# Sliding-window attention with routed experts: first loads on three queues, and the first expert tiles built earlier

## The chip, the core and the metric

The kernel runs on one core of a Trainium2 chip. A core has TensorE (matrix products; "PE" in the profile, its weight loads "PEld"), VectorE ("DVE"), ScalarE ("ACT"), GpSimd ("POOL") and SyncE ("SP", which here only starts transfers), each with its own instruction stream. They meet through semaphores. Sixteen DMA engines move data between the memory outside (HBM) and the on-chip memory. TensorE writes its products to PSUM, eight banks, from which VectorE or ScalarE copy them. The metric is the device time of one execution in microseconds (us). The kernel before takes 764.41 us, the median of 3 runs (762.5 to 765.28).

## What is computed

```python
# q, k, v: (8, 8, 576, 64); window 64
scores = q @ k.T / 8, kept where 0 <= query - key < 64
x = softmax(scores) @ v                    # -> (4608 tokens, 512)
logits = x @ w_gate                        # 8 experts
e = argmax(logits); gate = softmax(logits)[e]
y[t] = gate[t] * (relu(x[t] @ w1[e]) @ w2[e])   # w1[e] 512 x 1024, w2[e] 1024 x 512
```

Every token goes to one expert only. The kernel works in tiles of 256 tokens of one expert, so it must first know which tokens belong together, fetch their rows of x, and then multiply.

## The kernel before

Attention runs over 16 units (a pair of batches times a pair of heads), three steps each, so N = 48 steps. They are pipelined by hand: while the scores of one step are made, the softmax of the step before is transposed and the product with v of the step before that is under way.

```python
def step(s):
    prs[s + 1] = softened(*masked(s + 1, scored(s + 1)))   # scores (PE), mask and max (DVE), exp (ACT)
    px = weighted(s - 1, pTs.pop(s - 1))                   # times v (PE)
    ripe = logit(s - 3)                                    # x times w_gate (PE)
    pTs[s] = flipped(prs.pop(s))                           # transposes of the softmax (PE)
    divided(s - 1, px)                                     # by the row sums (DVE)
    if s % NST == 0:                                       # NST = 3: a new unit
        u = s // NST
        if u + 3 < NU and (u + 3) % NG == 0: load_rests((u + 3) // NG)
        load_v(u + 2); load_qk(u + 3)                      # loads, three units ahead
    turned(s + 3)                                          # transposes of q and k (PE)
    x_turned(s - 2)                                        # transposes of x (PE)
    for op in todo.pop(s, ()): op()                        # routing work placed by step
```

A sequence has 576 positions: 512 are read by `load_qk` and `load_v`, the last 64, for all heads at once, by `load_rests`. All of these go through SyncE's queue. Loads and steps begin like this:

```python
load_qk(0)
nc.sync.dma_start(out=wg[:, :, 0:E], in_=...)              # w_gate
nc.sync.dma_start(out=x_dram[NT : NT + 1, :], in_=zrow[:])
load_rests(0); load_v(0); load_qk(1); load_v(1); load_qk(2)
for g in range(NG):                                        # w1 of expert 0, in four parts
    step = NST * (g // 2) + g % 2 + 1
    todo.setdefault(step, []).append(partial(nc.scalar.dma_start, out=w1s[0][:, g : g + 1], in_=...))
for n, op in enumerate(left_sums(G, s1s[0], *w1q(0))):     # sums of blocks of w1, on GpSimd
    todo.setdefault(3 * NST + n, []).append(op)
# ...
for s in range(-3, N):
    step(s)
```

After each pair of batches (there are four) `choose` ranks the tokens within their experts on VectorE, `place` writes one-hots of a token's place (two VectorE instructions for each block of 128 tokens), `weigh` multiplies the rows of x by their gate, and `store` writes them to `x_dram`. The expert part then fetches rows from there. A table of places says which token stands where: TensorE multiplies the one-hots `lo` and `hi`, and the result is a list of row numbers. The whole table is ready only when the last pair is ranked. Two tiles of expert 0 are formed earlier, from the first three of the four pairs (27 of the 36 blocks):

```python
# in choose(), pair bg; last = 3, NE = 2, TB = 256
if bg == last - 1:
    V.tensor_scalar_max(count[:, 0:1], count[:, 0:1], float(NE * TB))

# the third pair's work by step; its first step is 39
for n in (0, 0, 1, 2, 2):
    do(n, part)                                            # the five parts of choose()
for m in range(NTB):                                       # NTB = 9 blocks
    do(3 + m // 3, partial(place, bg * NTB + m))
    do((2, 2, 3, 3, 4, 4, 4, 5, 5)[m], partial(weigh, bg, m, nc.scalar if m in (2, 6) else G))
    if m % ST == ST - 1:
        do(3 + m // ST, partial(store, bg, m // ST, G))
do(6, first_tiles)

def first_tiles():                                         # NJE = 27, C = 2
    V.scalar_tensor_tensor(out=key[:], ...)
    V.tensor_tensor(out=hi_e[:], in0=_inner(key[:], NE * C), in1=..., op=ALU.is_equal)
    slots = banks[next(tr_ring)](0, NE * C)
    for j in range(NJE):
        for i in range(2):
            nc.tensor.matmul(slots, lhsT=lo[:, i, j], rhs=hi_e[:, j], ...)
    V.tensor_scalar(out=perm_e[:], in0=slots, ...)         # row numbers of tiles 0 and 1
    gather_first(perm_e[:, 0:C])                           # zero, then an indirect transfer on GpSimd
```

After the last step, tile 0's products fill TensorE while VectorE ranks the last pair. A tile is `hidden` (seven groups of 16 products with w1; `a11` and so on are its blocks, combined so that seven block products do for eight), `turn` (transposes of the next tile's rows) and `output` (seven groups with w2); each `next` gives out one group:

```python
sums_w2(0)                                                 # sums of blocks of w2, on GpSimd
tile0 = chain(hidden(0), turn(), output(0))
px = weighted(N - 1, pTs.pop(N - 1))
form_all(turn())                                           # tile 0's own rows
logit(N - 3); divided(N - 1, px); x_turned(N - 2)
sums_x()
gather_first(perm_e[:, C : 2 * C])                         # tile 1's rows
by_tok = [by_tokens(last, c) for c in range(NST)]
next(by_tok[0]); next(tile0)
logit(N - 2); x_turned(N - 1); next(by_tok[0], None); next(by_tok[1]); next(tile0)
logit(N - 1); next(by_tok[2]); next(by_tok[1], None); next(tile0)
# ... choose(last) between the next groups, weigh_some, then
for _ in range(8):
    next(tile0)
    next(table, None)                                      # slot_table: the whole table of places
gather(perm_i[:, 3 * C : 4 * C])
finish(); scatter(perm_e[:, 0:C])
tile1 = chain(hidden(0), turn(), output(0))
```

`slot_table` multiplies the one-hots of the first 27 blocks, then writes those of the last nine block by block and multiplies them. All other tiles follow the same way, expert by expert.

Of the kernel before, what the change touches and what calls it, by code (L numbers as in the profile page):

```python
# [36 lines left out]
def kernel(  # L37
# [44 lines left out]

    ident = consts.tile([P, P], F32, name="ident")
    make_identity(nc, ident[:])
    GE = 32
# [127 lines left out]
    hi_e = rt.tile([P, NJE, NE * C], BF16, name="hi_e")  # L213
# [23 lines left out]
    ST = 3  # L237
# [39 lines left out]
    def gather_first(tokens):  # L277

        for c in range(C):
            G.memset(xg[c], 0.0)  # L280

            G.indirect_dma_start(
                out=xg[c], out_offset=None, in_=x_dram[0 : NT - BG * S, :],
                in_offset=bass.IndirectOffsetOnAxis(ap=tokens[:, c : c + 1], axis=0),
                bounds_check=NT - BG * S - 1, oob_is_err=False,
            )
# [12 lines left out]
    def turn():  # L299
# [7 lines left out]
    def sums_x():  # L307
# [132 lines left out]
    with tc.manual_schedule(), ExitStack() as held, ExitStack() as brief:  # L440
# [6 lines left out]


        NM = 2 + ST
        mask = consts.tile([P, NM, P], BF16, name="mask")  # L450
        nc.gpsimd.memset(mask[:], 0.0)
        for h in range(2):
            for m0, m1, first in ((0, 1, False), (1, 2, h == 0), (2, NM, False)):
                rows = slice(h * D, (h + 1) * D)
                sel = partial(
                    nc.gpsimd.affine_select, out=mask[rows, m0:m1, :], in_=mask[rows, m0:m1, :], fill=MASKED,
                )
                if first:
                    sel(pattern=[[0, m1 - m0], [-1, P]], compare_op=ALU.is_ge, base=0, channel_multiplier=1)
                else:  # L460
                    sel(pattern=[[0, m1 - m0], [1, P]], compare_op=ALU.is_gt, base=0, channel_multiplier=-1)
                    sel(pattern=[[0, m1 - m0], [-1, P]], compare_op=ALU.is_ge, base=WINDOW, channel_multiplier=1)
# [18 lines left out]
        def load_qk(u):  # L481
            bg, g = units[u]
            qks[u] = [qk_m(((u % 3 + 2) % 3 * 2 + n) * 1024, BG, NV, 2, D) for n in range(2)]
            for i in range(BG):
                for t, src in zip(qks[u], (q, k)):
                    for h in range(2):
                        nc.sync.dma_start(
# [4 lines left out]
        def load_rests(bg):  # L492

            at = 6144 + bg % 2 * 2048
            vr = qk_m(at + 1024, BG, H, D)
            rests[bg] = [qk_m(at, H, D), qk_m(at + 512, H, D), vr]
            for t, src in zip(rests[bg], (q, k)):
                for i in range(BG):
                    nc.sync.dma_start(
                        out=t[i * D : (i + 1) * D], in_=src[bg * BG + i, :, SM:S, :].rearrange("h p d -> p h d")  # L500
                    )
            for i in range(BG):
                nc.sync.dma_start(out=vr[D:P, i], in_=v[bg * BG + i, :, SM:S, :].rearrange("h p d -> p h d"))
# [173 lines left out]
        def choose(bg):  # L677
# [50 lines left out]
            if bg == last - 1:  # L728

                V.tensor_scalar_max(count[:, 0:1], count[:, 0:1], float(NE * TB))  # L730
# [48 lines left out]
        def slot_table(hi):  # L779
# [29 lines left out]
            for j in range(NJE):  # L809
                fill(j)  # L810
            for n in range(NST):
                for m in range(ST):
                    place(NJE + n * ST + m)
                yield
# [18 lines left out]
        def after(s, routing, bg):  # L833
# [14 lines left out]
            for n in (0, 0, 1, 2, 2):  # L848
                do(n, part)
            for m in range(NTB):  # L850
                do(3 + m // 3, partial(place, bg * NTB + m))
                do((2, 2, 3, 3, 4, 4, 4, 5, 5)[m], partial(weigh, bg, m, nc.scalar if m in (2, 6) else G))
                if m % ST == ST - 1:
                    do(3 + m // ST, partial(store, bg, m // ST, G))
            do(6, first_tiles)

        def first_tiles():

            V.scalar_tensor_tensor(
                out=key[:], in0=rkhi[:, 0:NJE], scalar=1.0, in1=oh_all[:, 0, 0:NJE], op0=ALU.add, op1=ALU.mult  # L860
# [209 lines left out]
```

## Time and profile before

| | |
|---|---|
| time, median of 3 runs | 764.41 us |
| span of the profiled execution | 763.5 us |
| TensorE busy | 722.8 us, 95% |
| VectorE, ScalarE, GpSimd busy | 397.0, 268.3 and 357.0 us |
| moved by DMA | 94.48 MB, of 137,616 packets 117,072 under 512 B |
| last score group of attention starts | 206.19 us |
| first product of tile 0, of tile 1 | 218.24 us, 249.66 us |

The profile is one execution in which each instruction has a start and a length. A line of the timeline gives the start, the length, the engine, the line of the kernel, the operation, what it writes and reads, its size, and in brackets how long the engine had been idle before it and what released it. Matmul ends are modelled, so a gap between two of them can be a little longer or shorter than it seems. Some lines of the kernel before to know: L572 is the scores, L539 and L531 the transposes of q and k (L531 those of the rests), L603 those of the softmax, L618 the product with v, L643 the transposes of x, L655 the logits, L869 the one-hots of the first tiles, L303 `turn`, L322 the products with w1, L362 those with w2, L807 the table of places.

### The profile page before, as it was taken

The page shows a single profiled execution, that of the slowest core. Times are in us where ns is not written, and L with a number is a line of the kernel's source. Part 1 is how long each engine was busy: PE and PEld are TensorE (multiplying, and loading weights), DVE is VectorE, ACT ScalarE, POOL GpSimd, SP SyncE. Part 2 cuts the span into 40 slices and gives each one's busy share as a digit, 9 for nine tenths or more (in the row PEclk, how much of TensorE's full clock was granted, in tenths as well). Part 3 has the DMA queues.
Part 4 walks back from the last instruction along what each step waited for, and adds up shares of the span by engine and source line. Part 5 has one row for each costly group of instructions (what it writes and reads, how often), then busy time and mean ns, then how long its engine had stood idle before and what let it go on. Part 6 is the DMA issues. An engine that isn't in the chain of part 4 may idle for free. (4 is left out here: it accounts for less than half of the span.)

```text
span 763.5 us, 18251 instructions
## 1 busy us (share of the span) xinstructions
PE 722.8 (95%) x7018; PEld 651.8 (85%) x7018; DVE 397.0 (52%) x1355; ACT 268.3 (35%) x676; POOL 357.0 (47%) x366
## 2 busy tenths in 40 slices
PE   5999999998899989999999999999999999999995
PEld 3878888887688978988999899899998899988994
DVE  2666998988748554434533452352434452424432
ACT  4778888897634201211220121111220121202220
POOL 5214668485770544546531553663256465262111
PEclk9999999999899999999999999999999999999998
DMA  7998889794513711702501170441161171101101
GB/s 161 210 201 183 190 183 257 175 236 128 181 56 125 276 57 32 264 29 93 203 32 54 48 257 30 141 164 56 44 247 53 35 258 56 41 25 42 43 28 55
DMA packets 137616, 94.48 MB, mean 124 GB/s; under 512 B 117072, under 2 KB 117072, under 8 KB 137490
## 3 DMA queue, kind: packets, MB, share of 16 engines
q1 hardware_dynamic: 127858, 62.16, 29.6%
q0 software_dynamic: 9056, 28.58, 11.3%
q10 hardware_dynamic: 576, 2.10, 0.9%
q8 instruction: 74, 1.21, 0.6%
q14 instruction: 52, 0.43, 0.2%
HBM read 73.94 MB, written 20.45 MB: 124 GB/s over the span
## 5 line engine op out<-in xcount | busy, mean ns | idle before, releaser
L322 PE MATMUL bank<-qk_m,s 128*128 128x128 f32 x1216 | 145.6, 275 | 0.0
L322 PEld LDWEIGHTS bank<-qk_m,s 128*128 128x128 f32 x1216 | 140.5, 192 | 0.1
L322 PE MATMUL bank<-qk_m,w 128*128 128x128 f32 x912 | 112.5, 276 | 10.7 <-DVE v_m L358 7.1
L272 POOL DMA_INDIRECT qk_m<-x_dram,at_g x42 | 44.6, 1061 | 166.3 <-PE bank L303 159.0
L322 PEld LDWEIGHTS bank<-qk_m,w 128*128 128x128 f32 x912 | 106.8, 192 | 15.9 <-issue 15.7
L595 ACT ACTIVATE pr<-pr,mx 128x128 f32<-128x128 f32 x288 | 89.7, 391 | 34.2 <-DVE mx L585 31.8
L358 DVE TENSOR_TENSOR v_m<-bank,v_m 128x256 f32<-128x256 f32 x101 | 40.9, 422 | 110.3 <-PE bank L362 54.8
L585 DVE CUSTOM_DVE_ANT_0 pr<-bank,mask 128x128 f32<-128x128 f32 x288 | 64.4, 286 | 28.2 <-PE bank L572 25.8
L292 POOL DMA_INDIRECT out_dram<-v_m,at_s x42 | 42.4, 1009 | 60.7 <-DVE v_m L358 49.0
L329 ACT COPY qk_m<-bank 128x512 f32<-128x512 f32 x19 | 11.2, 587 | 164.2 <-PE bank L322 135.0
L139 POOL TENSOR_TENSOR s<-w 128x1024 f32<-128x1024 f32 x22 | 52.3, 2377 | 17.6 <-DMA qk_m<-x_dram,at_g 17.6
L362 PE MATMUL bank<-qkT_m,v_m 128*128 128x256 f32 x240 | 54.0, 380 | 1.7 <-DVE v_m L139 1.7
L362 PEld LDWEIGHTS bank<-qkT_m,v_m 128*128 128x128 f32 x240 | 45.4, 190 | 8.6 <-DVE v_m L139 2.5
L513 POOL COPY v_m<-v_m 64x520 f32<-64x520 f32 x32 | 19.8, 618 | 69.3 <-DMA v_m<-in_v_dram 55.1
L362 PE MATMUL bank<-qk_m 128*128 128x256 f32 x224 | 52.1, 380 | 0.0
L618 PEld LDWEIGHTS bank<-v_m,pT 128*64 128x64 f32 x1152 | 41.2, 140 | 11.7 <-DVE xs L632 5.5
L618 PE MATMUL bank<-v_m,pT 128*64 128x65 f32 x1152 | 48.0, 231 | 2.7 <-DVE xs L632 2.7
L362 PE MATMUL bank<-s,v_m 128*128 128x256 f32 x216 | 48.1, 379 | 0.0
L362 PEld LDWEIGHTS bank<-qk_m 128*128 128x128 f32 x224 | 41.5, 190 | 5.5 <-ACT v_m L374 0.4
L362 PEld LDWEIGHTS bank<-s,v_m 128*128 128x128 f32 x216 | 41.0, 190 | 5.6
L572 PE MATMUL bank<-qkT_m 64*64 64x128 f32 x1152 | 45.4, 289 | 0.1
L539 PE MATMUL bank<-ident,qk_m 128*128 128x128 f32 x256 | 35.9, 283 | 8.5 <-DMA qk_m<-in_q_dram 6.3
(167 smaller groups left out, 1223.8 us busy)
## 6 DMA issues: line engine op xcount, KB each, us to landing
w<-in_moe_w_dram SPq DMA_DIRECT2D x11, 2048.0 KB, 9.4
qk_m<-in_q_dram SPq DMA_DIRECT2D x72, 128.0 KB, 3.4
qk_m<-in_k_dram SPq DMA_DIRECT2D x72, 128.0 KB, 3.4
v_m<-in_v_dram SPq DMA_DIRECT2D x64, 128.0 KB, 3.8
qk_m<-in_moe_w_dram SPq DMA_DIRECT2D x3, 2048.0 KB, 15.3
x_dram<-xs POOLq DMA_DIRECT2D x6, 512.0 KB, 4.7
x_dram<-xs POOLq DMA_DIRECT2D x3, 768.0 KB, 5.0
w<-in_moe_w_dram ACTq DMA_DIRECT2D x4, 512.0 KB, 4.4
```

The lines of the kernel that those rows point to most:

```text
L139: op()
L272: G.indirect_dma_start(out=xg[c], out_offset=None, in_=x_dram[:, :], in_offset=bass.IndirectOffsetOnAxis(ap=at_g[:, c : c + 1], axis=0),)
L292: put = G.indirect_dma_start(out=out[:, :], out_offset=bass.IndirectOffsetOnAxis(ap=at_s[:, c : c + 1], axis=0), in_=ys[c], in_offset=None ...
L322: nc.tensor.matmul(acc[:, f, :], lhsT=a[:, g, f * P : (f + 1) * P], rhs=b[:, g, :], start=(first and f == 0 and g == 0), stop=(g == HG - 1 ...
L358: plus = lambda out, a, b: V.tensor_tensor(out=out, in0=a, in1=b, op=ALU.add)
L362: nc.tensor.matmul(acc, lhsT=a[:, f, :], rhs=b[:, f, :], start=(start and f == 0), stop=(stop and f == HF - 1), skip_group_check=True,)
L513: nc.gpsimd.tensor_copy(out=vb[0:D, i].rearrange("p j h d -> p (j h d)"), in_=va[D:P, i].rearrange("p j h d -> p (j h d)"),)
L539: nc.tensor.transpose(out=tr.rearrange("d a b -> d (a b)").rearrange("d (p j) -> d j p", j=NV)[:, j, :], in_=t[:, c, j].rearrange("p h d - ...
L572: nc.tensor.matmul(out_, lhsT=qT[rows, t, a * WINDOW : (a + 1) * WINDOW], rhs=rhs, start=True, stop=True, skip_group_check=True,)
L585: V.tensor_tensor_reduce(out=prs[h][:, m, :], in0=scs[h][:, m, :], in1=mask[:, m0 + m, :], scale=-scale, scalar=-2 * MASKED, op0=ALU.add, ...
L595: nc.scalar.activation(out=y, in_=y, func=AF.Exp, scale=-1.0, bias=mx[:, h, m : m + 1])
L618: nc.tensor.matmul(px[a * D : (a + 1) * D, h, m, :], lhsT=pTs[h][:, m, a * D : (a + 1) * D], rhs=vt[:, h, :], start=True, stop=True, skip_ ...
```

## The change

It has four parts. **First loads:** the loads that open the kernel are ordered by first use and issued by three engines: SyncE, ScalarE (rests of q and k for the first two heads) and GpSimd (rests of the other heads). The opening steps are written out, so that the first scores stand ahead of the second block's transposes, and nine matmuls on zeros run before the first data is there. The masks are built sooner. **w1 of expert 0** is loaded in steps 13, 16, 19 and 22 rather than 1, 2, 4 and 5, and its sums follow in steps 24 to 27. **Tile 0** takes its tokens from the first two pairs of batches, tile 1 from the first three: each has its own one-hots, tile 0's in steps 38 and 39, tile 1's after the last step. Expert 0's count is raised to 256 after the second pair and to 512 after the third, so that a later token never gets a place in a closed tile. Ranking, placing, weighing and storing of the third pair are spread over steps 39 to 45, with the stores on SyncE. **Tile 0's rows** are turned in step 46 and its first product stands in step 47; in the slot table the products of the first 27 blocks come after the places of the sixth of the last nine.

The diff, cut to its core (the masks' code is only moved up; `turn` and `sums_x` take their banks as an argument):

```diff
+    warm = consts.tile([P, 4 * P], BF16, name="warm")
+    nc.vector.memset(warm[:], 0.0)
-    hi_e = rt.tile([P, NJE, NE * C], BF16, name="hi_e")
+    hi_e = rt.tile([P, NJE, C], BF16, name="hi_e")
-    def gather_first(tokens):
+    def gather_first(tokens, rows):
...
-                out=xg[c], out_offset=None, in_=x_dram[0 : NT - BG * S, :],
+                out=xg[c], out_offset=None, in_=x_dram[0:rows, :],
...
-            if bg == last - 1:
-                V.tensor_scalar_max(count[:, 0:1], count[:, 0:1], float(NE * TB))
+            if last - NE <= bg < last:
+                V.tensor_scalar_max(count[:, 0:1], count[:, 0:1], float((bg - last + NE + 1) * TB))
... slot_table
-            for j in range(NJE):
-                fill(j)
             for n in range(NST):
                 for m in range(ST):
                     place(NJE + n * ST + m)
+                if n == 1:
+                    for j in range(NJE):
+                        fill(j)
                 yield
... the third pair
-            for n in (0, 0, 1, 2, 2):
+            for n in (0, 1, 1, 2, 3):
                 do(n, part)
             for m in range(NTB):
-                do(3 + m // 3, partial(place, bg * NTB + m))
-                do((2, 2, 3, 3, 4, 4, 4, 5, 5)[m], partial(weigh, bg, m, nc.scalar if m in (2, 6) else G))
+                do((3, 3, 4, 4, 5, 5, 6, 6, 6)[m], partial(place, bg * NTB + m))
+                do((2, 3, 3, 4, 4, 5, 5, 6, 6)[m], partial(weigh, bg, m, G))
                 if m % ST == ST - 1:
-                    do(3 + m // ST, partial(store, bg, m // ST, G))
-            do(6, first_tiles)
+                    do(4 + m // ST, partial(store, bg, m // ST, nc.sync))
... first_tiles becomes first_tile(n), in two parts
+            nj = (last - NE + n + 1) * NTB                 # 18 blocks for tile 0, 27 for tile 1
+            gather_first(to, nj * P)
... the loads
-        load_qk(0)
+        load_qk(0, nc.sync, nc.sync)
+        load_rests(0, 0, 2, nc.scalar, nc.sync)
+        load_v(0)
+        load_qk(1, nc.sync, nc.sync)
+        load_rests(0, 2, H, G)
         nc.sync.dma_start(out=wg[:, :, 0:E], in_=moe_w_gate.rearrange("(g p) e -> p g e", p=P))
         nc.sync.dma_start(out=x_dram[NT : NT + 1, :], in_=zrow[:])
-        load_rests(0)
-        load_v(0)
-        load_qk(1)
         load_v(1)
-        load_qk(2)
+        load_qk(2, nc.sync, nc.sync)
-            step = NST * (g // 2) + g % 2 + 1
+            step = NST * (NG + g) + 1
...
-            todo.setdefault(3 * NST + n, []).append(op)
+            todo.setdefault(2 * NG * NST + n, []).append(op)
... in step(s): load_rests moves behind load_qk, to s % NST == 1, and
+            if s == 0:
+                turned(2)
... the last steps and the first
-        for n, s in enumerate((N - 6, N - 3)):
+        for n, s in enumerate((N - 7, N - 4)):             # w2 of expert 0
...
+        tile0 = chain(hidden(0), turn(), output(0))
+        first = first_tile(0)
+        todo.setdefault(N - 10, []).append(partial(next, first))
+        todo.setdefault(N - 9, []).append(partial(next, first))
+        free = [banks[i](0, NG, P) for i in (0, 1)]
+        todo.setdefault(N - 2, []).extend((lambda: form_all(turn(free)), partial(sums_x, free)))
+        todo.setdefault(N - 1, []).extend((partial(next, tile0), partial(sums_w2, 0)))
+        for _ in range(9):
+            nc.tensor.matmul(banks[7](0, 4 * P), lhsT=warm[:, 0:P], rhs=warm[:], start=True, stop=True)
+        turned(0)
+        first = masked(0, scored(0))
+        turned(1)
+        prs[0] = softened(*first)
-        for s in range(-3, N):
+        for s in range(N):
             step(s)
-        sums_w2(0)
... after the last step
-        form_all(turn())
...
-        sums_x()
-        gather_first(perm_e[:, C : 2 * C])
+        second = first_tile(1)
+        next(second)
+        next(tile0)
         by_tok = [by_tokens(last, c) for c in range(NST)]
         next(by_tok[0])
-        next(tile0)
         logit(N - 2)
         x_turned(N - 1)
+        next(second)
... and weigh_some(2) moves from before the last eight groups of tile 0 to after the second of them
```

## The prediction

> **What bounds the kernel now.** I read the slices of the page first, then a table of stages, then TensorE's timeline at the two ends of the attention half. The slices say who is busy:
>
> ```profile
> PE   5999999998899989999999999999999999999995
> PEclk9999999999899999999999999999999999999998
> DMA  7998889794513711702501170441161171101101
> ```
>
> TensorE (PE) is the bound nearly everywhere, so time can come back only where PE's row is below 9: slice 1, slices 10, 11 and 15 and the last (a slice is 19.1 us). Slice 11 also has a reduced clock. The diff touches slices 1 to 13. The stages in us (columns: window, its length, then busy time and count for PE, PEld, DVE, ACT, POOL; clock, DMA share, GB/s):
>
> ```profile
> 0.00:24.00 24.00, 15.22 (x138) 11.41 (x139) 7.41 (x53) 11.21 (x28) 9.77 (x36) 0.93 0.79 165
> 24.00:60.00 36.00, 34.40 (x611) 28.52 (x610) 24.12 (x144) 29.66 (x85) 8.51 (x18) 1.00 0.94 209
> 60.00:105.00 45.00, 44.88 (x794) 37.60 (x796) 38.25 (x209) 38.27 (x115) 25.64 (x35) 1.00 0.83 185
> 105.00:164.00 59.00, 58.36 (x1036) 48.87 (x1032) 52.76 (x291) 50.88 (x152) 40.07 (x51) 1.00 0.88 214
> 164.00:207.00 43.00, 37.48 (x688) 31.18 (x687) 37.05 (x195) 31.90 (x94) 29.53 (x35) 0.97 0.60 178
> 207.00:223.00 16.00, 14.49 (x183) 12.04 (x175) 6.72 (x28) 6.52 (x17) 13.52 (x9) 0.87 0.12 39
> ```
>
> PE is idle 8.8 us of the first 24, 1.6 of the next 36, next to nothing up to 164, then 5.5 in 164 to 207 and 1.5 in 207 to 223. These 17 us, and whatever runs at the slow clock inside "busy", are what the change can win. Attention has 48 steps, one score group (L572) each. In the quiet middle of the timeline two of three steps take 4.07 us and the third 3.42, so three cost 11.56 us, all of it PE work. The start falls short of that:
>
> ```profile
> 9.83 1.56 PE L572 MATMUL bank<-qkT_m 64*64 64x128 f32 x24
> ...
> 13.11 0.45 PE L531 MATMUL bank<-ident,qk_m 128*128 128x128 f32 x1 [1.10 <-DMA qk_m<-in_k_dram]
> 13.48 1.56 PE L572 MATMUL bank<-qkT_m 64*64 64x128 f32 x24
> ...
> 17.96 0.63 PE L539 MATMUL bank<-ident,qk_m 128*128 128x128 f32 x4 [1.44 <-DMA qk_m<-in_q_dram]
> ...
> 19.10 0.63 PE L539 MATMUL bank<-ident,qk_m 128*128 128x128 f32 x4 [0.51 <-DMA qk_m<-in_k_dram]
> ...
> 19.66 1.32 PE L572 MATMUL bank<-qkT_m 64*64 64x128 f32 x24
> ...
> 24.57 0.89 PE L572 MATMUL bank<-qkT_m 64*64 64x128 f32 x24
> ```
>
> The same group of 24 takes 1.56 us cold and 0.89 warm, and what releases the transposes is a load each time: first the rests (L531), then the second unit's q and k. The end of attention:
>
> ```profile
> 201.49 0.49 PE L643 MATMUL bank<-ident,xs 128*128 128x128 f32 x3
> 204.68 0.46 PE L869 MATMUL bank<-hi_e,lo 128*128 128x4 bf16 x12 [2.70 <-DVE hi_e L862]
> ...
> 206.19 1.56 PE L572 MATMUL bank<-qkT_m 64*64 64x128 f32 x24
> ...
> 215.58 0.97 PE L618 MATMUL bank<-v_m,pT 128*64 128x65 f32 x24 [0.88 <-DVE xs L632]
> 216.48 1.09 PE L303 MATMUL bank<-ident,qk_m 128*128 128x128 f32 x8
> ...
> 218.24 1.95 PE L322 MATMUL bank<-qk_m,w 128*128 128x128 f32 x16
> ```
>
> PE stands 2.70 us for the one-hots of the first two tiles, and the next scores run cold (1.56 instead of 0.89).
>
> **What the Trainium skill says.** "TensorE: Matmul & The Clock Gate", Part 1: the array starts at half clock, goes to full after a window of some 3.4 us of activity and falls back after an idle one. The trace agrees, 1.56 against 0.89 us for one group, at the start and again after the idle at 202 to 205. "DMA: Bandwidth & Descriptors", "Issuing engines are not separate DMA queues": several issuing engines share the same 16 DMA engines and save only issue time. The trace fits: a pair of loads costs SyncE 1.3 us of issue, while the DMA row is already at 7 to 9 tenths. "GPSIMD Engine Reference", Specifications: GpSimd shares its SBUF interfaces with VectorE. The DVE timeline agrees: the bf16 one-hot write (L746) takes 0.30 us alone and 0.73 to 0.81 in many places beside GpSimd's weighing (L757).
>
> **Part 1, the start.** Nine matmuls on zeros run before the first load is in; in the trace PE's first work waits until 4.63, so they cost nothing as long as they end by about 5. I expect 9 x 0.43 us (my estimate from 512 columns at the skill's cold 1.2 GHz) from about 1.2 to 5.1. They may or may not warm the array; PE then has holes again, so I count at most half of the cold loss (0.67 us per group on three groups) as won.
>
> The order of loads matters more. Before, the second unit's k for its first batch was released at 19.10, behind about 2.8 MB: q, k of unit 0 (1.0), rests of all heads (0.77), v (0.5), half of unit 1 (0.5). From the first DMA work at about 2.2 us that is 2.8 / 16.9 = 0.17 MB per us. The new order puts 0.19 MB of rests there instead of 0.77, so 0.58 MB less: 0.58 / 0.17 = 3.4 us earlier, 15.7. The rests of step 2 no longer precede the second scores (1.10 us and the block behind it), as their transposes move after the flip. So the third score group starts near 16.3 instead of 19.66, and I carry **3.5 us** plus 0.5 for clock to the fourth group: **4.0 us**.
>
> **Part 2, w1 later.** Four loads of 512 KB leave 24 to 45 us, where DMA is at 0.94 and the twelfth score step takes 5.44 instead of 4.07 because q and k of the next batch come late (1.4 us). They go to steps 13, 16, 19 and 22, some 65 to 105 us, where DMA has 0.83. At the 209 GB/s of the first stage 2 MB are 10 us of DMA time in 45, which fills that stage to about 1.05. I expect the 1.4 us to go and some to come back there: **0.5 us** net. The four sums on GpSimd (2.36 us each) move to steps 24 to 27, where GpSimd is at 40 of 59 us.
>
> **Part 3, steps 38 to 47.** Score groups 38 to 47 take 163.81 to 206.19, 42.4 us for nine steps; three times 11.56 is 34.7. The surplus of 7.7 us is 1.6 us of one-hot matmuls (54), 2.7 of waiting for hi_e, and DVE work packed into few steps (5.34, 5.70). After: the rank work is spread over five steps, the 18 pairs of place instructions over 2, 2, 2 and 3 a step instead of 3, 3, 3. Tile 0 uses two pairs of batches only, so its 36 one-hot matmuls stand in step 39 with inputs long ready: 36/54 of 1.6 = 1.04 us. DVE needs 8 x 2.6 us of base work, some 5 of ranks, 7 of places and 0.8 of keys, about 34 us, just under PE's 35.7, so I leave 2.5 us of waits. New: 34.7 + 1.0 + 2.5 = 38.2, **4.2 us less**.
>
> **Part 4, from the last scores to tile 1.** Before: last scores 206.19, last logits 222.84 (16.65 us), tile 1's first product 249.66. After, the turn of tile 0 (0.88), its first product (1.87) and the second tile's one-hots (1.6) stand between attention's last pieces. Sum: 4.07 and 4.25 for the two steps, then 0.9 + 0.35 + 0.42 + 1.87 + 0.35 + 0.42 + 1.6 + 0.1 + 1.8 = 16.1 us, warm and without holes; I take 16.5. From the logits on PE has one product less (1.87), and the hole of 1.29 us before the slot table's matmuls goes, as they move behind output products. But then DVE's chain (ranks, starts, table, places; VectorE is busy for 22.3 of the 27 us from 223 to 250) leads: about 25.4 us instead of 26.8. Together **1.5 us**.
>
> **Beyond 250 us** all is the same: 19 full and 2 half tiles before and after. The new floor on the first expert's count (256 after two pairs) does nothing: 421 of its tokens come in the first two pairs, 538 in three.
>
> **Sum.** 4.0 + 0.5 + 4.2 + 1.5 = 10.2 us; 764.4 - 10.2 = **754.2 us**, 1.3% less.
>
> **Rivals.** *DMA is the true bound of the first 60 us.* Then a start earlier by 4 us runs into the loads a few steps later and Parts 1 and 2 give 1 us. For: share 0.94 in 24 to 60. Against: 2 MB less to carry there, 10 us of DMA. Time: 758. *DVE's chain is the bound at the end.* Products pulled ahead of it cover less of it afterwards, so PE waits before tile 1 and Parts 3 and 4 give 2 us. For: DVE at 22.3 of 27 us. Against: 2.70 us of waiting and 2.2 us of cold clock go whatever follows. Time: 758. *A new wait.* GpSimd now weighs nine blocks (1.55 us each, 14 us), makes w2's sums (9.4 us) and only then gathers tile 1's rows. By my sums the gather lands some 21 us after the last scores and is wanted at 24. A few us late would cost the same on PE: 759, or 762 with another rival. *Everything works and the start stays warm:* up to 8 us at the start and 8 at the end: 748.
>
> **Range and chances.** Two rivals that halve one end each give 758; both together 761. The good case is 748, but needs PE without holes in 5 to 20 us, which loads at 0.17 MB per us hardly allow. So 749.5 to 760 for eight in ten. Over 2% faster means below 749.1, nearly the whole of what is idle: 0.09. Slower by 2% would need a stall of 25 us in a kernel whose instructions hardly change: 0.01. Within 2%: 0.90.
>
> **What would show it.** Right: nine warm matmuls ended by about 5 us; third scores near 16 us; fourth near 20.5; no 5.44 us step around 55; no wait for hi_e; the last scores 8 to 9 us earlier than 206.19; tile 1's first product near 239.5; from there to the end the same 514 us. Wrong: waits for loads in 20 to 60 or in 65 to 105 us; PE standing for DVE between the last logits and tile 1; transposes of tile 1 (L303's successor) waiting for the gather.

## The result and the profile after

The changed kernel takes 773.15 us, the median of 4 runs (769.4 to 775.55), against 764.18 us of the kernel before in the same comparison (4 runs, 762.5 to 765.28). The ratio is 1.0115, with a 95% interval of 1.0065 to 1.0164: it is about 9 us slower, where 10.2 us less had been predicted. The profiled execution spans 767.6 us, 4.1 more than before. It is the fastest of the four; a second profile further down spans 774.0.

The page's slices of the changed kernel, rows as before:

```profile
PE   7999999799799989999999999999999999999996
PEclk9999999999899999999999999999999999999999
DMA  8889899885404631611701171261161171011101
```

Slice 1 went from 5 to 7 tenths, but slices 8 (134 to 154 us) and 11 (192 to 211) now have a 7, where there were a 9 and an 8. The stages of the changed kernel (window, length, busy time and count of PE, PEld, DVE, ACT, POOL; clock, DMA share, GB/s):

```profile
0.00:24.00 24.00, 17.70 (x203) 11.88 (x204) 9.25 (x68) 13.78 (x36) 14.39 (x43) 0.94 0.87 175
24.00:60.00 36.00, 36.00 (x634) 30.37 (x635) 25.33 (x147) 30.55 (x90) 11.18 (x24) 0.99 0.82 179
60.00:105.00 45.00, 45.00 (x822) 38.20 (x822) 37.80 (x220) 39.00 (x117) 14.58 (x26) 1.00 0.90 205
105.00:164.00 59.00, 52.24 (x912) 43.26 (x908) 52.37 (x259) 44.48 (x133) 48.46 (x53) 1.00 0.89 210
164.00:207.00 43.00, 37.12 (x628) 30.77 (x626) 37.15 (x176) 29.79 (x89) 35.63 (x36) 0.92 0.64 196
207.00:223.00 16.00, 13.30 (x169) 10.62 (x165) 13.86 (x49) 7.03 (x20) 5.23 (x3) 0.89 0.01 2
```

Up to 105 us TensorE has fewer holes than before. Then it stands for 6.8 of the 59 us in which it had stood for 0.6, while GpSimd's busy time there rose from 40.1 to 48.5. In the last row VectorE is busy for 13.86 us instead of 6.72. TensorE's timeline at the start:

```profile
8.12 0.89 PE L575 MATMUL bank<-qkT_m 64*64 64x128 f32 x24 [0.68 <-ACT qkT_m L547]
...
9.96 1.46 PE L575 MATMUL bank<-qkT_m 64*64 64x128 f32 x24
...
15.26 0.89 PE L575 MATMUL bank<-qkT_m 64*64 64x128 f32 x24
...
20.13 0.63 PE L542 MATMUL bank<-ident,qk_m 128*128 128x128 f32 x4 [1.85 <-DMA qk_m<-in_k_dram]
20.69 1.13 PE L575 MATMUL bank<-qkT_m 64*64 64x128 f32 x24
```

The first and the fourth score group start at 8.12 and 20.69 instead of 9.83 and 24.57. In the middle and at the end of attention, where the changed kernel's L575 is the scores, L646 the transposes of x and L608 a copy of the softmax's transposes:

```profile
131.95 0.89 PE L575 MATMUL bank<-qkT_m 64*64 64x128 f32 x24
...
137.94 0.55 PE L646 MATMUL bank<-ident,xs 128*128 128x128 f32 x3 [2.17 <-DVE pT L608]
138.41 0.89 PE L575 MATMUL bank<-qkT_m 64*64 64x128 f32 x24
...
145.01 0.55 PE L646 MATMUL bank<-ident,xs 128*128 128x128 f32 x3 [2.78 <-DVE pT L608]
145.48 0.89 PE L575 MATMUL bank<-qkT_m 64*64 64x128 f32 x24
...
199.72 0.90 PE L646 MATMUL bank<-ident,xs 128*128 128x128 f32 x3 [4.10 <-DVE pT L608]
200.55 1.56 PE L575 MATMUL bank<-qkT_m 64*64 64x128 f32 x24
...
210.33 0.43 PE L575 MATMUL bank<-qkT_m 64*64 64x128 f32 x2 [0.91 <-DVE mx L588]
```

The wait for `hi_e` is gone, but TensorE now stands for VectorE: 2.17, 2.78 and 4.10 us, and after the last of these the scores run cold (1.56). A step is 6.46 and 7.07 us long where 4.07 is usual.

The length of each stage in us, from the starts of the score groups (counted from 0), for the profiles that the text speaks of; the names are those of the experiments below, "again" is the second profile of the changed kernel:

| | before | after | again | n | d | l | h | m |
|---|---|---|---|---|---|---|---|---|
| to group 3 | 24.57 | 20.69 | 19.85 | 20.65 | 20.26 | 20.75 | 20.59 | 20.58 |
| 3 to 29 | 103.67 | 101.80 | 107.88 | 102.34 | 105.32 | 107.00 | 106.68 | 102.87 |
| 29 to 33 | 15.80 | 22.99 | 23.49 | 17.61 | 15.80 | 15.73 | 15.77 | 15.71 |
| 33 to 38 | 19.77 | 19.64 | 19.29 | 20.93 | 20.11 | 20.67 | 21.87 | 21.94 |
| 38 to 47 | 42.38 | 45.21 | 43.64 | 43.75 | 41.76 | 42.42 | 39.20 | 39.46 |
| 47 to tile 1's first product | 43.47 | 45.39 | 46.18 | 45.10 | 43.47 | 42.94 | 44.13 | 44.11 |
| from there to the end | 513.9 | 511.9 | 513.7 | 513.4 | 511.0 | 512.0 | 513.5 | 511.9 |

Of the difference of 4.1 us between the first two columns, 5.8 us are won up to group 29, 7.2 lost in the four steps after it, 2.8 in groups 38 to 47 and 1.9 up to tile 1; 2.0 are won in the experts, where nothing was changed: this last row lies between 511.0 and 513.9 in all profiles and differs by 1.8 between the two of the changed kernel, so it is scatter.

What VectorE does while TensorE stands is the key. First VectorE, then GpSimd, of the changed kernel (L744 is a part of the ranking, L749 writes a one-hot of a place, L760 is the weighing):

```profile
132.85 3.10 DVE L719 TENSOR_SCALAR gate<-gate 128x9 f32<-128x9 f32 x1
...
136.12 0.23 DVE L588 CUSTOM_DVE_ANT_0 pr<-bank,mask 128x128 f32<-128x128 f32 x1
...
139.25 2.34 DVE L729 TENSOR_TENSOR r_rank<-r_inc,count 128x72 f32<-128x72 f32 x1
...
194.19 0.79 DVE L744 TENSOR_SCALAR r_half<-r_pos 128x9 int32<-128x9 int32 x1
...
199.76 0.19 DVE L632 RECIPROCAL rec<-rec 128x6 f32<-128x6 f32 x1
...
207.21 2.44 DVE L749 TENSOR_SCALAR lo<-lane,low,tok_b 128x128 bf16<-128x128 bf16 x1
```

```profile
133.54 2.37 POOL L930 TENSOR_TENSOR s<-w 128x1024 f32<-128x1024 f32 x1
...
139.14 2.37 POOL L930 TENSOR_TENSOR s<-w,s 128x1024 f32<-128x1024 f32 x1
...
185.56 14.01 POOL L760 TENSOR_SCALAR xs<-xs,gate 128x512 f32<-128x512 f32 x9
199.56 2.35 POOL L158 TENSOR_TENSOR qkT_m<-qk_m 128x1024 f32<-128x1024 f32 x1
...
207.24 2.36 POOL L158 TENSOR_TENSOR qkT_m<-qk_m 128x1024 f32<-128x1024 f32 x1 [2.30 <-PE bank L575]
```

L930 and L158 are GpSimd's sums of blocks of w1 and w2. L729 took 0.23 us before, L749 takes 0.30 to 0.31 alone; here they take 2.34 and 2.44. Start and length give the ends: 135.95 against 135.91 (L719), 141.59 against 141.51, 209.65 against 209.60. Each of these three small VectorE instructions, on 9 to 128 columns, ends with a GpSimd sum, within 0.1 us. The mask and the maxima (L588), queued behind, then keep TensorE waiting: 2.17, 2.78 and 0.91 us.

Not everything that VectorE does between tensors in SBUF is held. The reciprocal at 199.76 lies inside the sum of 199.56 and takes its usual 0.19 us; so do all 37 reciprocals of 128x6 that lie inside such a sum in the traces of this case (0.19 us each), and four reductions of 128x72 there take 0.23 to 0.29. The held ones are `TENSOR_TENSOR` and `TENSOR_SCALAR`.

The longest wait, 4.10 us, has another neighbour. It ends at 199.72, and up to 199.57 GpSimd weighs nine blocks, one input each. Beside them VectorE's ten instructions of ranks and places from 192.08 on (L737 to L749) take 6.28 us in all; the same ten take 2.42 us in the kernel h below, where GpSimd has nothing to do there (L744: 0.79 and 0.17), and TensorE's wait is 1.43 us. They are stretched to at most 0.96 us, less than a weighing (1.56).

### The profile page after: what moved, and what is told of

Same layout as the page of the kernel before. It is cut to its first block, busy times and chain, and to the rows that moved or that the text cites. A ratio compares the mean times of both kernels' runs of the same rounds, so it can differ in the third digit from the quotient of the medians.

```text
span 767.6 us, 18376 instructions
## 1 busy us (share of the span) xinstructions
PE 725.9 (95%) x7063; PEld 652.7 (85%) x7063; DVE 407.4 (53%) x1360; ACT 266.5 (35%) x674; POOL 360.9 (47%) x368
## 5 line engine op out<-in xcount | busy, mean ns | idle before, releaser
L598 ACT ACTIVATE pr<-pr,mx 128x128 f32<-128x128 f32 x288 | 89.4, 389 | 44.7 <-DVE mx L588 44.4
L588 DVE CUSTOM_DVE_ANT_0 pr<-bank,mask 128x128 f32<-128x128 f32 x288 | 64.2, 286 | 18.9 <-PE bank L575 17.8
L158 POOL TENSOR_TENSOR s<-w 128x1024 f32<-128x1024 f32 x22 | 52.4, 2381 | 19.0 <-DMA qk_m<-x_dram,at_g 18.9
L575 PE MATMUL bank<-qkT_m 64*64 64x128 f32 x1152 | 44.4, 282 | 1.9 <-DVE mx L588 1.1
L606 PE MATMUL bank<-ident,pr 128*128 128x128 f32 x288 | 44.4, 291 | 0.0
L760 POOL TENSOR_SCALAR xs<-xs,gate 128x512 f32<-128x512 f32 x27 | 42.1, 1569 | 0.6
## 6 DMA issues: line engine op xcount, KB each, us to landing
w<-in_moe_w_dram ACTq DMA_DIRECT2D x4, 512.0 KB, 4.9
x_dram<-xs POOLq DMA_DIRECT2D x4, 512.0 KB, 5.2
```

The costliest lines, as they stand in the source:

```text
L575: nc.tensor.matmul(out_, lhsT=qT[rows, t, a * WINDOW : (a + 1) * WINDOW], rhs=rhs, start=True, stop=True, skip_group_check=True,)
L588: V.tensor_tensor_reduce(out=prs[h][:, m, :], in0=scs[h][:, m, :], in1=mask[:, m0 + m, :], scale=-scale, scalar=-2 * MASKED, op0=ALU.add, ...
L598: nc.scalar.activation(out=y, in_=y, func=AF.Exp, scale=-1.0, bias=mx[:, h, m : m + 1])
L606: nc.tensor.transpose(out=tr[:, m, :], in_=prs[h][:, m, :], identity=ident[:])
L760: engine.tensor_scalar(out=y, in0=y, scalar1=s, scalar2=None, op0=ALU.mult)
```

## Experiments

The theory (P in the recorded texts): a two-input GpSimd instruction holds VectorE's small instructions between tensors in SBUF until it ends; the change moved GpSimd's sums to where VectorE ranks and places tokens. Rivals: **D**, the later loads of w1 collide with q, k and v; **O**, tile 0's pieces, put in before attention ends, cost more than they bring; **V**, VectorE simply has too much to do. In the recorded texts the first experiment is a, the second b. Ratios are to the kernel before, with 95% intervals.

**f: the kernel before, with the four sums of w1 in steps 24 to 27.** No transfer and no other instruction is moved.

```diff
-            todo.setdefault(3 * NST + n, []).append(op)
+            todo.setdefault(2 * NG * NST + n, []).append(op)
```

> The kernel before with one line changed: the four sums of w1's blocks on GpSimd stand in steps 24 to 27 instead of 9 to 12; the loads of w1 stay early, so no transfer moves. Theory P: the second pair's ranking in steps 27 to 31 meets them, and the time rises by 4 to 8 us, to 768 to 772. Theory D: within 1 us of 764, as it is the loads that matter. A result near 764 would say that the sums alone do not do it.

Measured: 768.72 us (5 runs, 766.99 to 769.48), ratio 1.0059 (1.0037 to 1.0081). Groups 29 to 33 take 19.18 us instead of 15.80. One line, about half of the whole loss, without any load moved: P, not D.

**i: the changed kernel, with the four sums of w1 on VectorE, in steps 26, 33, 35 and 37.** The loads stay late.

```diff
-        for n, op in enumerate(left_sums(G, s1s[0], *w1q(0))):
-            todo.setdefault(2 * NG * NST + n, []).append(op)
+        for n, op in zip((26, 33, 35, 37), left_sums(V, s1s[0], *w1q(0))):
+            todo.setdefault(n, []).append(op)
```

> The kernel after with only the four sums of w1 moved from GpSimd to VectorE in steps 26, 33, 35 and 37; loads late, weighing on GpSimd, w2's sums not held. Theory P: steps 30 to 33 go from 23 to about 16 us and the rest stays: 765 to 768. Theory D: no change, 772 to 774, since the loads stay where they are. This tells sums from loads in the changed kernel, as the sums moved alone did in the kernel before.

Measured: 768.44 us (10 runs, 764.94 to 776.22), 1.0079 (1.0046 to 1.0111). VectorE has 4 x 1.22 = 4.9 us more to do, and yet groups 29 to 33 take 16.68 us instead of 22.99. That speaks against V. The interval of the ratio overlaps the changed kernel's, so it is this stage that shows it, not the time. Groups 38 to 47 stay slow (45.96), as the weighing and w2's sums are still on GpSimd there.

**n and o: one input instead of two, and the changed kernel again.** In n each sum of w1 becomes a product of one block with 1.0, on GpSimd, in the same step and with the same output size; the sums are left out, so expert 0's output lacks them. o is the changed kernel itself.

```diff
-        for n, op in enumerate(left_sums(G, s1s[0], *w1q(0))):
-            todo.setdefault(2 * NG * NST + n, []).append(op)
+        for n, a in enumerate((w1q(0)[2], w1q(0)[0], w1q(0)[0], w1q(0)[1])):
+            todo.setdefault(2 * NG * NST + n, []).append(
+                partial(G.tensor_scalar, out=s1s[0][:, n], in0=a, scalar1=1.0, scalar2=None, op0=ALU.mult))
```

> The changed kernel with w1's four sums of expert 0 on GpSimd in the same steps 24 to 27, but each replaced by a product of one block with 1.0: the same output size, one input instead of two (the sums are left out, so expert 0's result is wrong by that). By the weighing's 1.56 us for 128 x 512 I expect each to take 3.1 us, longer than the 2.36 us of a sum. If it is the second input that holds VectorE's SBUF work, no VectorE instruction of 2.3 to 3.1 us stands beside them, they are only stretched 2 to 4 times, the loss of 7.2 us in steps 30 to 33 falls to some 2, and the time to about 769. If it is GpSimd's load as such (later stores, a later queue), the time is 773 or more, as these take 3 us longer in all.

> The changed kernel once more, beside the one with one-input products, so that both stand on the same chip: 772 to 774 if the four executions of the first comparison were typical of it.

Measured on the same chip: n 765.98 us (11 runs, 763.47 to 771.02), 1.0036 (1.0015 to 1.0056); o 774.09 us (5 runs, 770.98 to 775.81), 1.0127 (1.0099 to 1.0154). So 8.1 us less, although GpSimd works longer: its products take 2.77 us each, its sums 2.36. VectorE and then GpSimd of n, at the same instructions as above:

```profile
133.13 0.17 DVE L719 TENSOR_SCALAR gate<-gate 128x9 f32<-128x9 f32 x1
...
136.32 0.95 DVE L725 TENSOR_TENSOR_SCAN r_inc<-keep,r_ranks 128x72 f32<-128x72 f32 x1
137.30 0.23 DVE L729 TENSOR_TENSOR r_rank<-r_inc,count 128x72 f32<-128x72 f32 x1
```

```profile
136.04 2.79 POOL L932 TENSOR_SCALAR s<-w 128x1024 f32<-128x1024 f32 x1
```

L729 lies wholly inside GpSimd's 2.79 us and takes 0.23; only the instruction ahead of it is stretched, to 0.95 (0.30 in the kernel before). So it is the second input, not GpSimd's load, that holds. The 8.1 us are more than the 5.4 that n wins in groups 29 to 33 against the first profile. The second profile of the changed kernel shows another loss, of some executions only. TensorE and then ScalarE of o, around the fourth load of w1 (ACTq is the issue of a transfer, L598 the exponential, L606 and L608 the softmax's transposes and their copies):

```profile
109.77 1.57 PE L621 MATMUL bank<-v_m,pT 128*64 128x65 f32 x22 [2.86 <-ACT pT L608]
```

```profile
107.06 0.34 ACTq L930 DMA_DIRECT2D w<-in_moe_w_dram  x1
107.50 1.86 ACT L598 ACTIVATE pr<-pr,mx 128x128 f32<-128x128 f32 x6 [4.33 <-DVE mx L588]
```

ScalarE ended its last copy at 103.16 and did nothing until it issued this load at 107.06 and then the exponentials, although the last of their maxima had been ready at 105.17; this step took 9.96 us instead of 4.07. In j's profile ScalarE is idle for 3.26 us around the same load; in the other seven profiles with the loads in steps 13 to 22 the idle time there is 1.3 us or less. So D holds a part that the first profile doesn't show; how often it comes isn't known from these runs.

**a: the changed kernel, with w1's loads and sums where they were before.**

```diff
-            step = NST * (NG + g) + 1
+            step = NST * (g // 2) + g % 2 + 1
...
-            todo.setdefault(2 * NG * NST + n, []).append(op)
+            todo.setdefault(3 * NST + n, []).append(op)
```

> The kernel after with one part undone: w1 of expert 0 is loaded in steps 1, 2, 4 and 5 and its four sums stand in steps 9 to 12, as before. Theory P (VectorE's small SBUF instructions are held while GpSimd's two-input sums run): steps 30 to 33, 23 us after the change, go back to about 16, the instructions of 3.10, 2.34 and 1.65 us in the second pair's ranking go back to 0.2 to 0.3, and the time falls by some 6 us, to 765 to 768, less what the earlier sums cost where they now stand. Theory D (the time goes to DMA): the loads come back to 20 to 45 us, waits for q and k return there (1 to 3 us), and the gain is less than 4 us. Theory O (tile 0's work inside the last steps lengthens TensorE's path): no more than 2 us.

Measured: 769.97 us (11 runs, 766.01 to 777.7), 1.008 (1.006 to 1.0101). Groups 29 to 33 are back at 15.80, and yet 769.97 is far from the kernel before; the interval even overlaps the changed kernel's. Early in attention ScalarE is idle for 3.09 and 2.19 us around the issue of these loads (once in the kernel before, 2.09), but that can't be what is left: d below has the same loads and the same opening, with 3.12 and 2.28 us, and is faster than before. What is left lies with the third pair's weighing and w2's sums, as g below shows, where both are dealt with.

**b: the changed kernel, with the third pair's rows weighed on VectorE.** This was my first idea for steps 38 to 47, when I took the weighing for the cause.

```diff
-                do((2, 3, 3, 4, 4, 5, 5, 6, 6)[m], partial(weigh, bg, m, G))
+                do((2, 3, 3, 4, 4, 5, 5, 6, 6)[m], partial(weigh, bg, m, V))
```

> The kernel after with one engine changed: the nine weighings of the third pair go to VectorE instead of GpSimd. Theory P: GpSimd is nearly still in steps 41 to 45, so ranking and places lose their stretched instructions; TensorE's wait of 4.10 us for VectorE near 195 us goes, with the cold clock that followed. VectorE gets 9 x about 0.35 us = 3 us more work (0.35 is an estimate from its 0.55 us for 384 elements read from PSUM; SBUF may be faster). Net 5 to 8 us faster than after, 765 to 768. Theory D: no change, as no transfer moves. Theory V (VectorE is simply full there): slower by up to 3 us.

Measured: 775.27 us (4 runs, 774.78 to 776.95), 1.0153 (1.0125 to 1.0182). No gain. VectorE weighs a block in 0.47 to 0.48 us, GpSimd in 1.56; but with GpSimd empty, w2's sums no longer stand behind the weighing in its stream and start earlier, amid ranks and places. VectorE and GpSimd of b:

```profile
195.88 2.39 DVE L742 TENSOR_SCALAR r_half<-r_pos 128x9 int32<-128x9 int32 x1
...
208.95 2.42 DVE L749 TENSOR_SCALAR lo<-lane,low,tok_b 128x128 bf16<-128x128 bf16 x1
```

```profile
195.87 2.36 POOL L158 TENSOR_TENSOR qkT_m<-qk_m 128x1024 f32<-128x1024 f32 x1 [6.79 <-ACT qkT_m L547]
...
208.96 2.35 POOL L158 TENSOR_TENSOR qkT_m<-qk_m,qkT_m 128x1024 f32<-128x1024 f32 x1 [10.73 <-PE bank L575]
```

A 9-column instruction takes 2.39 us. TensorE's waits beside these are 3.64 and 3.88 us. The weighing had been a plug ahead of the sums: one neighbour of VectorE's chain was exchanged for another, and groups 38 to 47 take 45.97 us.

**j: the changed kernel, with w2's sums held back.** GpSimd copies one element of the third pair's last one-hot before the sums, which makes them wait for the places.

```diff
-        todo.setdefault(N - 1, []).extend((partial(next, tile0), partial(sums_w2, 0)))
+        todo.setdefault(N - 1, []).extend((
+            partial(next, tile0), partial(G.tensor_copy, out=scr[:], in_=lo[:, 1, NJE - 1, 0:1]), partial(sums_w2, 0)))
```

> The kernel after with only w2's sums held until the last place is written; weighing stays on GpSimd, w1's sums in steps 24 to 27. Theory P: the wait of 4.10 us near 195 us stays, as it stands beside the weighing, and the place instruction of 2.44 us near 207 us goes; 1 to 3 us faster than after, 770 to 772. If nothing moves, the sums of w2 were not on the path in this kernel, only in the one with the weighing on VectorE.

Measured: 766.63 us (7 runs, 765.07 to 771.35), 1.0048 (1.0029 to 1.0066). That is 6.5 us less than the changed kernel, where 1 to 3 were expected, from the order of two pieces of GpSimd's work; it doesn't add to the 8.1 of n, as the whole loss is 9. In the profile groups 38 to 47 take 43.51 us instead of 45.21, and the stretch from 47 to tile 1's first product 42.36 instead of 45.39. The wait beside the weighing stays, as expected: 3.56 us.

**g and h: both sets of sums away from VectorE's chains.** g is a with b's weighing and j's hold; h is i with b's weighing and j's hold. All of tile 0's pieces are in both.

> The kernel after with three edits: w1 early again (as in the first experiment), the third pair's weighing on VectorE (as in the second), and GpSimd's sums of w2's blocks held until the last place of the third pair is written, by a copy of one element of that place ahead of them. In the second experiment VectorE still stood four times for 2.3 to 2.4 us, each time beside one of these sums. Theory P: with no two-input GpSimd work beside ranking and places, steps 43 to 47 lose their waits; last scores near 200 us instead of 206.3 (first experiment); time 763 to 765, that is 5 to 7 us under the first experiment's 769.97. Theory O (tile 0's pieces in the last steps are what costs): no faster than 768. Theory V (VectorE is simply full): 766 to 770.

> The kernel after with w1 loaded late as the change has it, but its four sums on VectorE in steps 26, 33, 35 and 37 (about 1.1 us each, an estimate from 0.68 us for 512 elements of the same kind), with the third pair's weighing on VectorE and w2's sums held as in the run before. Theory P: both stalls of the change go and its opening keeps its 5.7 us; 755 to 760, faster than before. Theory D (w1's loads at 65 to 105 us cost): 765 or more, as they stay. Theory V: VectorE 8 us fuller, 762 to 766.

Measured: g 760.75 us (20 runs, 758.97 to 764.77), 0.9963 (0.9952 to 0.9975); h 761.78 us (20 runs, 758.08 to 765.33), 0.997 (0.9953 to 0.9986). Both are faster than before with tile 0's pieces in place, which speaks against O as the main cause. Groups 38 to 47 take 38.70 us in g and 39.20 in h, where 38.2 was predicted; with b's weighing alone they take 45.97, with j's hold alone 43.51. So both neighbours of VectorE have to go, the weighing and the sums. g lies 9.2 us below a.

**d and l: without tile 0's pieces.** d is the kernel before with the opening alone; l is d with w1's loads late and its sums on VectorE, as in i. l against h shows what the early tile is worth with the late loads, d against g with the early ones; l against d shows what the late loads, with their sums on VectorE, are worth.

> The kernel before with the opening of the change alone: the loads by three engines in order of use, the nine matmuls on zeros, the opening steps written out, the rests a step later. w1 stays in steps 1, 2, 4 and 5, all of routing and tile 0 as before. If the opening is a true gain, the fourth score group starts near 20.7 us instead of 24.57 and 2 to 4.5 us remain at the end: 760 to 762. If DMA is the bound of the first 60 us, w1's loads give the gain back as waits for q and k: 763 to 764. If an earlier start only shifts which GpSimd work meets which VectorE work, the end can move by a few us either way.

> The kernel before with the opening, the late loads of w1 and its four sums on VectorE in steps 26, 33, 35 and 37; nothing of the tile 0 parts. If the early tile is worth what it was meant to be once GpSimd stays away from VectorE's chains, this must be some 4 us slower than the kernel with all four parts and the same sums (761.8): 764 to 766. If the early tile is worth nothing, it is the same or better: 759 to 762, with the last scores near 203 to 204 and tile 1's first product near 247.

Measured: d 761.24 us (20 runs, 758.71 to 764.47), 0.9964 (0.9953 to 0.9975); l 764.36 us (22 runs, 760.56 to 766.22), 1.0005 (0.9994 to 1.0015). The opening is worth 3 us by itself. Between l and h lie 2.6 us, less than the 4 expected, for the early tile with b's weighing and j's hold; l still stands 2.71 us for `hi_e`. But between d and g lie only 0.5 us (0.9964 and 0.9963), so that the early tile is worth anything isn't shown. And l is 3.1 us slower than d: moving w1's loads and sums does not pay even when GpSimd makes no sums of w1. At first it does: l reaches group 11 at 51.01 us, d at 54.86. Then l's step from group 28 to 29 takes 10.55 us, where d's takes 4.15. The reason can be read in h as well. VectorE of h, where L635 is the division that writes `xs`:

```profile
120.55 0.56 DVE L635 TENSOR_TENSOR xs<-bank,rec 128x384 f32<-128x384 f32 x1 [3.41 <-DMA x_dram<-xs]
```

and GpSimd of h, where L516 puts v together and L760 is the weighing:

```profile
109.15 0.62 POOL L516 COPY v_m<-v_m 64x520 f32<-64x520 f32 x1 [3.50 <-DMA v_m<-in_v_dram]
...
112.05 1.56 POOL L760 TENSOR_SCALAR xs<-xs,gate 128x512 f32<-128x512 f32 x1
```

The division waits for a buffer of `xs` that an earlier chunk's store still reads; the stores wait for GpSimd's weighing, and this stands in GpSimd's stream behind copies that wait for v. In l the same wait is 3.82 us, and the pair's first store is issued at 114.34; in d there is no such wait, and the store is issued at 109.51. The DMA share from 95 to 110 us is 1.03 in l and 0.85 in d, so that v comes late because of w1's loads is likely, but it wasn't tested by itself. The wait stands in all eight profiles with late loads in which GpSimd weighs the first two pairs, its longest between 1.36 us (i) and 4.10 (b), and in none of the others.

**m: h, with the weighing of the first two pairs on VectorE too.**

```diff
-                    do(5 + m * 2 // 3, partial(weigh, bg, m, G))
+                    do(5 + m * 2 // 3, partial(weigh, bg, m, V))
```

> The kernel of 761.8 us (w1's sums and the third pair's weighing on VectorE, w2's sums held) with the weighing of the first two pairs on VectorE too, so that GpSimd's slow weighing no longer delays their stores. If the division's wait for a store near 120 us (3.4 us, with the step of 10.1 us) is a cost of GpSimd's lag, it goes, and the last scores come 3 to 4 us earlier, near 200.5: 757 to 759. If VectorE is simply full in these steps, 18 more instructions of 0.45 us (8 us) take the gain back or more: 762 to 766.

Measured: 760.72 us (22 runs, 758.57 to 764.92), 0.9962 (0.9951 to 0.9974). In the profile the wait for the store is gone and the last scores start at 200.56, where 200.5 was expected. The time missed its range of 757 to 759: against h (0.997) the intervals overlap, so the gain isn't shown. The profiled execution was the fastest of m's 22, and spans differ by some us from one execution to the next.

## Why the prediction was wrong

**Part 1 was right.** The nine matmuls on zeros ran from 1.27 to 4.78, and the first three score groups took 0.89, 1.46 and 0.89 us instead of 1.56, 1.56 and 1.32. The third group starts at 15.26 (16.3 predicted) and the fourth 3.88 us earlier (4.0). d, with this part alone, keeps 3 us of it.

**Part 2 failed at "the four sums on GpSimd move to steps 24 to 27, where GpSimd is at 40 of 59 us".** That asks whether GpSimd has room. It has; VectorE does not have room for GpSimd's second input. Instead of 0.5 us won, 7.2 were lost in groups 29 to 33 (f: 3.4 from this alone; i and n: gone, mostly, with it). The first half of the part, on transfers, was right, and more than predicted: with the same opening, group 11 starts at 50.95 to 52.78 us with the late loads and at 54.86 to 57.51 with the early ones (a, d, g). But later the late loads bring VectorE's wait for a store, up to 4.10 us, and ScalarE's stand at a load, which early loads have too, still comes in some executions (o, j).

**Part 3 failed at "about 34 us, just under PE's 35.7, so I leave 2.5 us of waits".** The 34 us left out what GpSimd does beside VectorE. In the changed kernel VectorE is busy for 39.4 of the 45.2 us. The prediction itself named the shared interface and read it as a stretch from 0.30 to 0.73 to 0.81 (24 of the 72 one-hot writes before are stretched, to between 0.32 and 0.96), but put no such stretch into its sum: in one step the weighing turns 2.42 us into 6.28, and TensorE stands 4.10 us, where it stands 1.43 in h. On top of that w2's sums hold VectorE to their end. With both away from VectorE's chain, g takes 38.7 us, h 39.2 and m 39.5, against 38.2. That this is so close is partly luck: VectorE is busy for 34.3 us in g, but 3.1 of these are seven weighings that the sum didn't have; the places take 4.9 instead of 7; and the 8 x 2.6 us of base work should have been nine for nine steps.

On the hold, the Trainium skill, "SBUF — State Buffer", section "Who interferes with whom", calls the ports that the two engines share an exclusive lock, and says that a VectorE instruction with two SBUF inputs contends with a GpSimd instruction that reads SBUF. It also counts `tensor_scalar`, as in L719 and L749, among those that can take the ports. The runs agree beside sums (0.23 became 2.34, 0.30 became 2.44). The division of n, which reads PSUM, is not held: it takes its usual 0.56 us at 195.74 beside a sum from 195.65 to 197.99, and the place behind it 1.83. The runs don't agree that the one that comes second always waits for the whole instruction: beside the 2.79 us product with one input, L729 took 0.23.

**Part 4 was half right.** From the last logits to tile 1's first product 25.0 us (25.4 predicted). From the last scores to the last logits 20.4 instead of 16.5. The term that was mis-sized is "4.07 and 4.25 for the two steps": in m it is 11.5 us, from 200.56 to the product with v at 212.03. It left out tile 0's first product of 2.02 us, which stands in the second of these steps, and waits of 0.48, 0.25, 0.70 and 0.40 us for VectorE. So this part costs 0.6 us in g, h and m (44.1 against 43.5), where 1.5 was to be won. Only in j's profile, where the two steps take 9.7 us, is it won in part (42.4).

**Rivals and range.** "A new wait" was listed, with GpSimd as its source, but as tile 1's gather landing late. The gather wasn't it: tile 1's turn at 239.24 waits for nothing. "Slower by 2% would need a stall of 25 us in a kernel whose instructions hardly change" put nothing above 760 in the range: what changes is which instructions of two engines stand beside each other, and the changed kernel and h, which differ in little else, are 11 us apart.

**What stays open.** How often ScalarE's stand comes; why L719 was held from 132.85, 0.7 us before the sum started, when GpSimd was issuing stores (the same 3.10 to 3.11 us in o and j, but 2.38 in b, where it starts with the sum). Why one-input work stretches VectorE's instructions and two-input work holds them. What the early tile is worth. A version with early loads and all weighing on VectorE wasn't tried. The best three (g, m, d) are within 0.5 us of each other, 0.4% faster than before.

## What to carry to other kernels

Before moving work to an engine with idle time, look at what will run beside it: for GpSimd instructions with two SBUF inputs, list VectorE's `TENSOR_TENSOR` and `TENSOR_SCALAR` instructions between SBUF tensors in the same stretch and count up to a whole GpSimd instruction for each meeting, or give the sums to VectorE. Work with one input costs too: count VectorE's chain beside it at its stretched length (6.28 us instead of 2.42 here). Taking work off GpSimd may also let what stands behind it start at a worse moment, so hold that too. Buffers that are freed by the moved engine's later work are part of the same question.

## What the runs showed of the hardware

- Beside a 128x1024 two-input GpSimd instruction (2.35 to 2.37 us), a small VectorE `TENSOR_TENSOR` or `TENSOR_SCALAR` between SBUF tensors ended with it in all cases shown: 128x9 in 3.10 and 2.39 us, 128x72 in 2.34, 128x128 bf16 in 2.44. A reciprocal of 128x6 inside it took its usual 0.19. The sums themselves keep their length beside these small instructions (2.35 to 2.37); beside VectorE's own 128x512 sums in the experts they take up to 2.81 us.
- Beside GpSimd instructions with one input VectorE's were not held as long: L729 took 0.23 us inside a 128x1024 product of 2.79 us, and ten instructions beside the weighing took 6.28 us instead of 2.42, none of them more than 0.96.
- VectorE makes the same sum in 1.22 us, and weighs a 128x512 block in 0.47 to 0.48 us where GpSimd takes 1.56.
- ScalarE was idle for up to 2.09 us (before), 3.12 (d), 3.26 (j) and 4.33 (o) around the issue of one 512 KB load; in o the exponentials behind it start 2.33 us after the last of their maxima was ready.
